# Scores of two heads in nearly every place of an attention loop, with values beside them

## The chip, the cores and the metric

The kernel runs on one core of a Trainium2 chip. The metric is the device time of one execution, in microseconds (us). The kernel before takes 1787.1 us (median of 3 runs, 1787.08 to 1787.36). Smaller is better.

## What is computed

Eight batches of attention with 12 heads, 448 tokens and 64 values per head, then a feed-forward block. Everything is float32 at the surface.

```python
scores = (q @ k.T) / 8                         # per batch and head, 448 x 448
scores = einsum('bhij,hg->bgij', scores, w_pre)    # heads mixed before the softmax
attn = exp(scores - max); attn /= sum + 1e-9
attn = einsum('bhij,hg->bgij', attn, w_post)       # heads mixed after it
x = (attn @ v), heads side by side             # 3584 tokens x 768
h = x @ w_in                                   # 2048 wide
out = (h - tanh(h)) @ w_out
```

The heads are mixed before and after the softmax, so all 12 heads of a token must be together twice: once for `w_pre`, once for `w_post`.

## The kernel before, in words

The attention part is one long loop over **places** (`for p in range(NPL + 3)`, L832; 180 of them). A batch is cut into four **blocks** of query tokens (120, 120, 120 and 88), 32 blocks in all. A block is cut into **groups** of 10 tokens with their 12 heads (120 rows of 128); a place handles two groups.

In every place TensorE (PE) does the same frame. **Premix** (`premix`, L513, matmuls L521) multiplies the gathered scores of the two groups with `w_pre` into the two PSUM banks of `ps_p`. **Mix** (`mix`, L548, matmuls L560) multiplies the exponentials of the place before with the scaled `w_post` into the two banks of `ps_o`, of which there is one copy only. Around these stand: VectorE (DVE) takes the row maximum (L530); ScalarE (ACT) the exponential with the row sum (L532); DVE forms the reciprocal of the sums (`norm`, L541 and L542) and GpSimd (POOL) scales `w_post` by it (`wr`, L543); ACT copies the mixed result to `at` at the start of the next place (L570, or L577 in two pieces where the two groups belong to different blocks or differ in size).

Between premix and mix a place may have **jobs**, from the table `todo`:

- `scores` (L467, matmuls L477): the scores of one **pair** of heads of a later block, 6 matmuls into two banks of `ps_m`; ACT copies one head to `s`, DVE the other (L482). Six pairs make a block.
- `values` (L590, matmuls L602): half of a finished block's `at` times v, 48 instructions into one bank of `ps_m`; DVE copies the result to `x` (L620). It needs all of the block's `at`.
- `prep_q` (L435, transposes L443): three transposes of q for a later block into one bank; ACT rounds them (`qh`, L456), DVE takes the rest (`ql`, L458). Two of these per block.
- `prep_k` (L409, transposes L417): four transposes of k into one bank; ACT (`kk`, L428) and DVE (L429) copy. Six per batch.
- `load_k`, `load_v`, `load_q`: entries in a list of DMAs that SyncE (SP) issues in later places.

`ps_m` has four banks in all. The order of a place's jobs on PE is fixed by `rank`: transposes, values, scores. On ACT and DVE a job's copies come behind the place's exponentials or row maxima; of DVE's, the score copies first, then what `then` and `last` hold (the rest of k and q, then the copy to `x`).

At the end of most places a few steps of the **narrowing** of the feed-forward weights are put in (`narrow_chunk`, L71; `Steps`, L113): 11 steps per chunk on DVE (L80 to L94), ACT (L82, L85, L102) and POOL (L96, L98, L104), 56 chunks. In ACT's order they stand between a place's score copies and the copy of the mix.

The rows of the scores reach the premix by a **gather** (L507, DMA L510): 120 rows of `s` from token order to group order, two per place, issued two places ahead, in a ring of six tiles.

All five engines run the instructions strictly in the order in which the code lists them (`in_order`). So the table `todo` sets what stands where. In the kernel before, each job of `scores` in the planner's list is two pairs, and the planner puts one job, scores or values, in a place, taking the other kind next where both are due. `prep_q` goes one place ahead of the block's first scores, both halves together; `prep_k` where no scores and no `prep_q` stand.

Behind the loop the feed-forward part streams the narrowed weights, with three matmuls per product of rounded parts (L257, L258, L262, L302 to L305). The change does not touch it.

## Time and profile before

| | |
|---|---|
| median of 3 runs | 1787.1 us |
| the profiled execution itself | 1788.9 us |
| its span, first to last instruction | 1787.2 us |
| mean granted TensorE clock | 0.993 |
| PE busy | 1751.0 us |
| DVE, ACT, POOL busy | 1128.3, 1000.5, 320.1 us |
| places of the attention loop | from 26.4 to about 838 us |

A row of the groups names line, engine, operation, output and inputs, the count, then the busy time and the mean of one, then the engine's idle time just before these instructions and what released it. A row of the timeline begins with start and duration in us; `x8` says how many instructions are merged; the bracket at its end is idle time before it and the releaser. A row of the windows has the stretch, its length, then busy time and count for PE, its weight loads, DVE, ACT and POOL, then the granted clock, the DMA share and GB/s. A float32 matmul is two instructions on PE in the trace and one row in the program's order; the ends of matmuls are modelled, so a section's cost is best read from start to start.

### The profile page before, as it was taken

To read this page: it belongs to the slowest core of one execution; us is meant where nothing else is said; L and a number is where in the kernel's file an instruction comes from. 1 tells how busy PE (TensorE), PEld (TensorE's weight loads), DVE (VectorE), ACT (ScalarE), POOL (GpSimd) and SP (SyncE) were. 2 spreads that over 40 slices of the span, in tenths; PEclk is the share of its full clock that TensorE was granted. 3 is DMA by queue.
4 is the path that set the end of the run, shared out by engine and by line. 5 is a ranking of instruction groups with operands and counts; after the bars stand their busy time and mean duration, and the time that the engine had idled before them with its cause. 6 is when DMAs were issued, how large, how long until landed. Compare 5 with 4: busy or idle time off the path is not lost.

```text
span 1787.2 us, 41382 instructions
## 1 busy us (share of the span) xinstructions
PE 1751.0 (98%) x16572; PEld 1425.6 (80%) x16572; DVE 1128.3 (63%) x2362; ACT 1000.5 (56%) x2051; POOL 320.1 (18%) x417
## 2 busy tenths in 40 slices
PE   8999999999999999999999999999999999999998
PEld 6777777777777777777888888888888888888887
DVE  5676777777777767664556566565565565655555
ACT  5777877777777776765343443433434434444333
POOL 1333333333333333321010010000000000000000
PEclk9999999999999999999999999999999999999999
DMA  8668687777967687565655655655656655655651
GB/s 176 204 196 216 194 236 224 217 215 215 249 203 218 215 213 220 178 202 216 255 207 194 248 193 207 241 193 214 229 197 216 224 208 204 228 217 190 230 194 36
DMA packets 232816, 372.32 MB, mean 208 GB/s; under 512 B 98992, under 2 KB 207536, under 8 KB 218288
## 3 DMA queue, kind: packets, MB, share of 16 engines
q1 hardware_dynamic: 231740, 368.45, 64.0%
q8 instruction: 131, 2.15, 0.5%
q10 hardware_dynamic: 884, 1.22, 0.2%
q14 instruction: 61, 0.50, 0.1%
HBM read 245.37 MB, written 47.19 MB: 164 GB/s over the span
## 4 chain that ended last, share of the span: by engine, by line
PE 87%; DMA 4%; ACT 4%; DVE 3%; issue 1%; POOL 0%; SPq 0%; ACTq 0%; DVEq 0%; POOLq 0%
PE ps_o L560 13%; PE ps_h L257 8%; PE ps_h L258 8%; PE ps_h L262 8%; PE ps_m L602 8%; PE ps_p L521 7%; PE ya L305 6%; PE ya L302 6%; PE ya L303 6%; PE ps_q L477 5%; PE yb L305 3%; PE yb L303 3%; PE yb L302 3%; DMA t<-s 2%; PE ps_m L443 1%
## 5 line engine op out<-in xcount | busy, mean ns | idle before, releaser
L560 PEld LDWEIGHTS ps_o<-wr,e 60*112 60x112 f32 (+1 forms) x5760 | 306.2, 176 | 44.3 <-POOL wr L543 21.8
L560 PE MATMUL ps_o<-wr,e 60*112 60x60 f32 (+1 forms) x5760 | 315.5, 259 | 14.3 <-POOL wr L543 7.7
L530 DVE TENSOR_REDUCE mx<-ps_p 128x1 f32<-128x448 f32 x360 | 207.7, 619 | 163.9 <-PE ps_p L521 163.7
L532 ACT ACTIVATE e<-ps_p,mx 128x448 f32<-128x448 f32 x360 | 225.7, 634 | 101.9 <-DVE mx L530 99.4
L289 ACT CAST gh<-r 128x512 fp32r<-128x512 f32 x112 | 69.6, 621 | 372.6 <-DVE r L282 372.6
L258 PE MATMUL ps_h<-xl,w 128*128 128x512 f32 x672 | 264.4, 393 | 0.0
L257 PE MATMUL ps_h<-xh,w 128*128 128x512 f32 x672 | 264.3, 393 | 0.0
L570 ACT COPY at<-ps_o 112x960 f32<-112x960 f32 x156 | 153.7, 985 | 93.8 <-PE ps_o L560 93.2
L247 POOL TENSOR_TENSOR xl<-rx,xh 128x512 fp32r<-128x512 f32 x38 | 55.6, 1464 | 731.2 <-ACT xh L246 731.2
L521 PE MATMUL ps_p<-t,wpre 60*64 60x448 f32 (+1 forms) x1440 | 180.8, 569 | 3.9 <-DMA t<-s 2.7
L305 PE MATMUL ya<-w,gl 128*128 128x512 f32 x448 | 177.0, 395 | 0.7 <-DVE gl L290 0.7
L278 DVE SCALAR_TENSOR_TENSOR r<-qa,ps_h 128x512 f32<-128x512 f32 x112 | 77.1, 688 | 159.2 <-ACT t L275 159.2
L302 PE MATMUL ya<-w,gh 128*128 128x512 f32 x448 | 174.8, 390 | 1.0 <-ACT gh L289 1.0
L303 PE MATMUL ya<-w,gh 128*128 128x512 f32 x448 | 174.8, 390 | 0.0
L602 PEld LDWEIGHTS ps_m<-at,vr 112*64 112x64 f32 x3072 | 147.5, 137 | 31.0 <-ACT at L577 10.9
L262 PE MATMUL ps_h<-xh,w 128*128 128x512 f32 x672 | 170.6, 389 | 0.0
L602 PE MATMUL ps_m<-at,vr 112*64 112x120 f32 (+1 forms) x3072 | 161.6, 261 | 8.4 <-ACT at L577 3.1
L272 ACT ACTIVATE u<-ps_h 128x512 f32<-128x512 f32 x112 | 67.0, 599 | 152.9 <-PE ps_h L262 152.9
L262 PEld LDWEIGHTS ps_h<-xh,w 128*128 128x128 f32 x672 | 126.3, 188 | 26.3
L258 PEld LDWEIGHTS ps_h<-xl,w 128*128 128x128 f32 x672 | 127.5, 190 | 23.7
L257 PEld LDWEIGHTS ps_h<-xh,w 128*128 128x128 f32 x672 | 127.4, 190 | 23.4
L543 POOL TENSOR_TENSOR wr<-wpost,zs 128x120 f32<-128x120 f32 x180 | 70.2, 390 | 402.9 <-DVE zs L542 293.6
(93 smaller groups left out, 3038.0 us busy)
## 6 DMA issues: line engine op xcount, KB each, us to landing
w<-ws SPq DMA_DIRECT2D x112, 1536.0 KB
t<-s SPq DMA_DIRECT2D x342, 210.0 KB
cr<-in_moe_w_in_dram SPq DMA_DIRECT2D x24, 512.0 KB
cr<-in_moe_w_out_dram SPq DMA_DIRECT2D x32, 384.0 KB
vr<-in_v_dram SPq DMA_DIRECT2D x24, 448.0 KB
kr<-in_k_dram SPq DMA_DIRECT2D x23, 448.0 KB
out_dram<-ob SPq DMA_DIRECT2D x24, 384.0 KB
qr<-in_q_dram SPq DMA_DIRECT2D x23, 360.0 KB
```

What stands on the lines that cost most here:

```text
L257: nc.tensor.matmul(ph, wh[:, fs], xh, start=(c == 0), stop=False)
L258: nc.tensor.matmul(ph, wh[:, fs], xl, start=False, stop=False)
L262: nc.tensor.matmul(ph, wl[:, fs], xh, start=False, stop=(c == NK - 1))
L302: nc.tensor.matmul(y, gh[:, tok], wh[:, es], start=first, stop=False)
L303: nc.tensor.matmul(y, gh[:, tok], wl[:, es], start=False, stop=False)
L305: nc.tensor.matmul(y, gl[:, tok], wh[:, es], start=False, stop=last)
L521: nc.tensor.matmul(pss[r][halves[j], :], wpre[k, :], ts[j][k, :], start=True, stop=True)
L530: nc.vector.tensor_reduce(out=mx, in_=ps, axis=AX.X, op=ALU.max, negate=True)
L532: nc.scalar.activation(e, ps, AF.Exp, bias=mx, scale=1.0, accum_out=zs[:, 0, r : r + 1])
L560: nc.tensor.matmul(ps[:CP, j, c * GP : (c + 1) * GP].rearrange("p (h i) -> p h i", i=GI)[:, :, r * GH : (r + 1) * GH], e[k, c * CP : (c + ...
L570: nc.scalar.copy(ats[i0][:, :, :, at : at + 2 * GI].rearrange("p c h (j i) -> p j (c h) i", j=2), ps[:CP, :, : NC * GP].rearrange("p j (x ...
L602: nc.tensor.matmul(pv[j * D : (j + 1) * D, r, :n], vt[:, j, c, :], ats[i][:, c, 2 * hp + j, :n], start=(c == 0), stop=(c == NC - 1),)
```

## The change

The planner that fills `todo` is rewritten. Scores are now placed pair by pair: for each block the pairs that are left are divided by the places that are left until they are due, rounded up. Values go into a place with no scores, or into one with one pair where the last values are two places back. The first blocks of a batch (but the very first) get their values two places later than the others. Transposes go wherever fewer than four banks of `ps_m` are taken; the two halves of `prep_q` may stand in different places. The first load of v for a batch waits until the place behind the last values of the batch before.

```diff
-        halved = []
+        def banks(p):
+
+            return sum({scores: 2, values: 1, prep_q: 1, prep_k: 1}.get(f, 0) for f, *a in todo[p])
+
+        at_s, at_v = {}, {}
+        due_s, due_v = [], []
         for i in range(len(blocks)):

             f0, f1, f2 = first[i : i + 3]
             if i + 1 < len(blocks):
-                lo = max(0, (f0 - 1) // 2 - 1)
-                hi = f1 // 2 - 3
-                for x in range(0 if i else 1, 3):
-                    e = lo + 2 * x if lo + 4 <= hi else lo + (hi - lo) * x // 2
-                    halved.append((e if i else x - 1, hi, "s", i + 1, x))
-            for x in range(2):
-                halved.append(((f1 - 1) // 2 + 2, f2 // 2 + 1 if f2 < NG else NPL + 7, "v", i, x))
...
+                lo, hi = max(0, (f0 - 1) // 2 - 1), f1 // 2 - 3
+                due_s += [(lo, hi, i + 1, hp) for hp in range(0 if i else 2, NP)]
+
+            lo = (f1 - 1) // 2 + (4 if i and i % NM == 0 else 2)
+            due_v += [(lo, f2 // 2 + 1 if f2 < NG else NPL + 7, i, x) for x in range(2)]
+        p, apart = 0, 2
+        while due_s or due_v:
+            now_s = 0
+            if due_s and due_s[0][0] <= p:
+                _, hi, i, _ = due_s[0]
+                left = sum(x[2] == i for x in due_s)
+                assert p <= hi, (p, hi, i)
+                now_s = -(-left // (hi - p + 1))
+                for _ in range(now_s):
+                    _, _, i, hp = due_s.pop(0)
+                    at_s[i, hp] = p
+                    at_place(p, scores, i, hp)
+            if due_v and due_v[0][0] <= p:
+                _, hi, i, x = due_v[0]
+                assert p <= hi, (p, hi, i)
+                if p + (1 - x) >= hi or now_s == 0 or now_s == 1 and apart >= 2:
+                    due_v.pop(0)
+                    at_v[i, x] = p
+                    at_place(p, values, i, x)
+                    apart = 0
+            apart += 1
             p += 1
...
             if b and m == 0:
+
+                p = max(p0 + 4, at_v[i - 1, 1] + 1)
+                assert p + 4 < at_v[i, 0], (p, at_v[i, 0])
                 for hq in range(NP // 2):
-                    at_place(p0 + 4 + hq, load_v, b, hq)
+                    at_place(p + hq, load_v, b, hq)
...
                 for r in range(2):
-                    while any(f is scores or f is prep_q for f, *a in todo[o]):
+                    while banks(o) > 3:
                         o += 1
                     at_place(o, prep_k, b, 2 * hq + r)
...
+        last_q = 0
+        for i in range(len(blocks)):
+            if i + 2 < len(blocks):
+                p = at_s[i + 2, 0]
+                for t in (1, 0):
+                    p -= t
+                    while banks(p) > 3:
+                        p -= 1
+                    at_place(p, prep_q, i + 2, t)
```

What this moves is read from the order of the instructions. The first place is PE in places 28 and 29, the start of the second batch. Before:

```order
L521 MATMUL ps_p<-t,wpre 64x448 x4
L417 MATMUL ps_m<-ident,kr 128x112 x8
L560 MATMUL ps_o<-wr,e 112x12x5 x16
L521 MATMUL ps_p<-t,wpre 64x448 x4
L477 MATMUL ps_q<-kk,qh 120x448 x4
L477 MATMUL ps_q<-kk,ql 120x448 x2
L477 MATMUL ps_q<-kk,qh 120x448 x4
L477 MATMUL ps_q<-kk,ql 120x448 x2
L560 MATMUL ps_o<-wr,e 112x12x5 x16
```

And with the change:

```order
L521 MATMUL ps_p<-t,wpre 64x448 x4
L417 MATMUL ps_m<-ident,kr 128x112 x8
L477 MATMUL ps_q<-kk,qh 120x448 x4
L477 MATMUL ps_q<-kk,ql 120x448 x2
L560 MATMUL ps_o<-wr,e 112x12x5 x16
L521 MATMUL ps_p<-t,wpre 64x448 x4
L477 MATMUL ps_q<-kk,qh 120x448 x4
L477 MATMUL ps_q<-kk,ql 120x448 x2
L560 MATMUL ps_o<-wr,e 112x12x5 x16
```

One of the two pairs (a row of four and a row of two matmuls) has moved ahead by a place, beside the k transposes; places 30 and 31 are then like 29, with one pair each and no values, where before place 30 had values.

The second is PE in places 18 and 19, where the third block of the first batch has just been mixed. Before:

```order
L521 MATMUL ps_p<-t,wpre 64x448 x4
L560 MATMUL ps_o<-wr,e 112x12x5 x16
L521 MATMUL ps_p<-t,wpre 64x448 x4
L477 MATMUL ps_q<-kk,qh 120x448 x4
L477 MATMUL ps_q<-kk,ql 120x448 x2
L477 MATMUL ps_q<-kk,qh 120x448 x4
L477 MATMUL ps_q<-kk,ql 120x448 x2
L560 MATMUL ps_o<-wr,e 112x12x5 x16
```

With the change:

```order
L521 MATMUL ps_p<-t,wpre 64x448 x4
L477 MATMUL ps_q<-kk,qh 120x448 x4
L477 MATMUL ps_q<-kk,ql 120x448 x2
L560 MATMUL ps_o<-wr,e 112x12x5 x16
L521 MATMUL ps_p<-t,wpre 64x448 x4
L602 MATMUL ps_m<-at,vr 64x120 x24
L477 MATMUL ps_q<-kk,qh 120x448 x4
L477 MATMUL ps_q<-kk,ql 120x448 x2
L560 MATMUL ps_o<-wr,e 112x12x5 x16
```

The empty place 18 has got a pair, and the values, which stood in place 20 behind six q transposes, now stand in 19, directly behind the premix and ahead of a pair.

The third is DVE in a place with values and q transposes. Before (place 43):

```order
L530 TENSOR_REDUCE mx<-ps_p 128x1 x2
L80 TENSOR_SCALAR cm<-cr 128x384
L458 SCALAR_TENSOR_TENSOR ql<-ps_m,qh 128x3x120 x2
L620 COPY x<-ps_m 128x3x12x10
L541 TENSOR_SCALAR zs<-zs 128x1 x2
L542 RECIPROCAL zs<-zs 128x2
```

With the change (place 42):

```order
L530 TENSOR_REDUCE mx<-ps_p 128x1 x2
L482 COPY s<-ps_q 120x448
L89 SCALAR_TENSOR_TENSOR cr<-cm,cs 128x384
L94 TENSOR_SCALAR cs<-cr 128x384
L458 SCALAR_TENSOR_TENSOR ql<-ps_m,qh 128x3x120
L620 COPY x<-ps_m 128x3x12x10
L541 TENSOR_SCALAR zs<-zs 128x1 x2
L542 RECIPROCAL zs<-zs 128x2
```

A score copy, which waits for matmuls that stand behind the values, has come ahead of the narrowing, `ql`, `x` and the sums. The narrowing's steps are at the same places in both kernels.

More of the change, by code (lines that the diff above doesn't have):

```diff
@@ L760, in kernel_body @@
             if i + 1 < len(blocks):
-                lo = max(0, (f0 - 1) // 2 - 1)
-                hi = f1 // 2 - 3
-                for x in range(0 if i else 1, 3):
-                    e = lo + 2 * x if lo + 4 <= hi else lo + (hi - lo) * x // 2
-                    halved.append((e if i else x - 1, hi, "s", i + 1, x))
-            for x in range(2):
-                halved.append(((f1 - 1) // 2 + 2, f2 // 2 + 1 if f2 < NG else NPL + 7, "v", i, x))
-        at_s, p, kind = {}, 0, None
-        while halved:
-            ready = sorted((x for x in halved if x[0] <= p), key=lambda x: (x[1], x[3:]))
-            if ready:
-                x = ready[0]
-                assert p <= x[1], (p, x)
-                other = [y for y in ready if y[2] != kind]
-                if x[2] == kind and other and x[1] > p + 1:
-                    x = other[0]
-                halved.remove(x)
-                _, _, kind, i, n = x
-                if kind == "s":
-                    at_s[i, n] = p
-                    for hp in (2 * n, 2 * n + 1):
-                        at_place(p, scores, i, hp)
-                else:
-                    at_place(p, values, i, n)
+                lo, hi = max(0, (f0 - 1) // 2 - 1), f1 // 2 - 3
[23 more added lines that the diff above has]
+            apart += 1
             p += 1
@@ L788, in kernel_body @@
             p0 = first[i] // 2
-            if i + 2 < len(blocks):
-                p = at_s[i + 2, 0] - 1
-                at_place(p, prep_q, i + 2, 0)
-                at_place(p, prep_q, i + 2, 1)
-                if i + 3 < len(blocks):
-                    at_place(p + 1, load_q, i + 3)
             if b and m == 0:
+                p = max(p0 + 4, at_v[i - 1, 1] + 1)
+                assert p + 4 < at_v[i, 0], (p, at_v[i, 0])
                 for hq in range(NP // 2):
-                    at_place(p0 + 4 + hq, load_v, b, hq)
+                    at_place(p + hq, load_v, b, hq)
         for b in range(1, B):
@@ L807, in kernel_body @@
                 if hq > KB - 4:
-                    o = max(o, at_s[blocks.index((b - 1, 3)), hq - 1 - (KB - 4)] + 1)
+                    o = max(o, at_s[blocks.index((b - 1, 3)), 2 * (hq - 1 - (KB - 4)) + 1] + 1)
                 for r in range(2):
-                    while any(f is scores or f is prep_q for f, *a in todo[o]):
+                    while banks(o) > 3:
                         o += 1
@@ L814, in kernel_body @@
                 done.append(o)
-                assert o < at_s[blocks.index((b, 0)), hq], (b, hq)
+                assert o < at_s[blocks.index((b, 0)), 2 * hq], (b, hq)
+        last_q = 0
[7 more added lines that the diff above has]
+                    at_place(p, prep_q, i + 2, t)
+                    last_q = max(p, last_q) if t == 0 else p
+                assert p > at_s.get((i, NP - 1), 0), p
+                p = last_q
+                if i + 3 < len(blocks):
+                    at_place(p + 1, load_q, i + 3)
         rank = {prep_k: 0, prep_q: 0, values: 1, scores: 2}
         for x in todo.values():
-            x.sort(key=lambda job: rank.get(job[0], 3))
+            x.sort(key=lambda job: (rank.get(job[0], 3), job[2] if job[0] is prep_q else 0))
         def hidden_0():
```

## The prediction

> **What bounds the kernel now.** I read the page first, then the groups of TensorE's instructions, then a window over the places of the attention loop, then the timeline of single places.

> ```profile
> PE 1751.0 (98%) x16572; PEld 1425.6 (80%) x16572; DVE 1128.3 (63%) x2362; ACT 1000.5 (56%) x2051; POOL 320.1 (18%) x417
> PE 87%; DMA 4%; ACT 4%; DVE 3%; issue 1%; POOL 0%; SPq 0%; ACTq 0%; DVEq 0%; POOLq 0%
> ```

> TensorE (PE) is the engine of the chain: 98% busy, 87% of the chain. The change adds and removes no matmul, so it can only move PE's waits, the little that a section costs to start, and the clock. The waits are in the window of the 180 places, which the change rewrites; everything behind it (the feed-forward part, about 950 us) is untouched.

> ```profile
> 26.41:838.20 811.79, 788.23 (x11556) 609.74 (x11556) 569.35 (x1538) 601.13 (x1371) 256.87 (x348) 0.99 0.72 211
> ...
> L560 PE MATMUL ps_o<-wr,e 60*112 60x60 f32 (+1 forms) x5760 | 315.5, 259 | 14.3 <-POOL wr L543 7.7 <-ACT at L570 6.0 <-POOL cl L104 0.3
> L521 PE MATMUL ps_p<-t,wpre 60*64 60x448 f32 (+1 forms) x1440 | 180.8, 569 | 3.9 <-DMA t<-s 2.7 <-ACT at L570 1.0
> L602 PE MATMUL ps_m<-at,vr 112*64 112x120 f32 (+1 forms) x2976 | 157.7, 262 | 8.4 <-ACT at L577 3.1 <-ACT at L570 2.7 <-DMA vr<-in_v_dram 2.4
> ```

> In 811.8 us PE is idle 23.6 us. By group (the rows of the attention part, idle before each): 14.3 us before the mix, 8.4 before the values, 3.9 before the premix (its first 1.6, and a little at the end, lie outside the window). That is all there is to win, a little over 1% of the time, and the same three lines are where a loss would stand.

> A place with four heads of scores, then an empty one, on PE (start, duration):

> ```profile
> 510.17 0.98 PE L521 MATMUL ps_p<-t,wpre 60*64 60x448 f32 x8
> 511.09 0.67 PE L477 MATMUL ps_q<-kk,qh 64*120 64x448 f32 x4
> ...
> 511.79 0.56 PE L477 MATMUL ps_q<-kk,qh 64*120 64x448 f32 x4
> ...
> 512.40 1.69 PE L560 MATMUL ps_o<-wr,e 60*112 60x60 f32 x32
> 514.02 0.98 PE L521 MATMUL ps_p<-t,wpre 60*64 60x448 f32 x8
> 516.34 1.78 PE L560 MATMUL ps_o<-wr,e 60*112 60x60 f32 x32 [1.33 <-POOL wr L543]
> 518.05 0.98 PE L521 MATMUL ps_p<-t,wpre 60*64 60x448 f32 x8
> ```

> From start to start: premix 0.92, first pair of heads 0.70, second pair 0.61, mix 1.62; the whole place 3.85. In the empty place behind it the mix could have begun 0.99 after the premix (516.34 - 514.02 less the wait of 1.33) and lasts 1.71: PE has 2.70 of work there and took 4.03.

> **The change part by part.**

> *PE's own work.* A place with one pair (two heads) should take 0.92 + 0.70 + 1.62 = 3.24. The program order has 92 places with two pairs before; with the change 26 with two and 131 with one. Scores: 131 x 0.70 + 26 x 1.31 - 92 x 1.31 = +5.2. The mix behind scores is 0.09 shorter than behind nothing or behind values, in 65 more places: -5.9. Only 3 of 14 empty places stay (premix 0.07 shorter elsewhere): -0.8. Split transposes start some 20 more sections; between 0 and the 0.09 by which a first pair exceeds a second, I take 0.05: +1.0. Sum -0.5, which I count as 0. If a lone pair cost 0.61 it would be -12; at 0.75, +6.5. The first pair is the nearest row, so 0.

> *The mix in the old light places.* 23 places without values behind another such place (13 empty, 10 with two k transposes) carry nearly all of the 14.3 us, 0.62 each. Each gets one pair, 0.70 later mix: those below that wait nothing, the 1.33 above and a 1.50 at 107.5 (below) keep 0.6 and 0.8, and two or three more like them keep some. I leave 4.5: **-9.8**. Bounds -14.3 and -6.

> *New light places behind light places.* The program order now has 50 of them, 27 more, because scores that stood alone between values places have been spread over all. What limits such a place is ScalarE (ACT), which works in order:

> ```profile
> 513.18 0.96 ACT L482 COPY s<-ps_q 120x448 f32<-120x448 f32 x2
> ...
> 517.03 0.51 ACT L102 CAST cs<-cm 128x384 fp32r<-128x384 f32 x1
> 517.43 0.53 ACT L82 ACTIVATE cm<-cm 128x384 f32<-128x384 f32 x1
> 517.85 0.55 ACT L85 ACTIVATE cr<-cr 128x384 f32<-128x384 int32 x1
> 518.29 0.96 ACT L570 COPY at<-ps_o 112x960 f32<-112x960 f32 x1
> ```

> The score copies start 3.01 after the place's premix (513.18 - 510.17), once both exponentials are through. One copy is 0.48, so ACT is free at 3.49, 0.25 into the next place of 3.24. The narrowing of the weights then takes 0.42 per operation (517.03 to 517.43 to 517.85), and the copy of the last mix 0.96 plus 0.1 to hand over (an estimate here and below): done 1.31 + 0.42 n into the place. PE wants to mix at 1.62. So n = 0 waits nothing, n = 1 0.1 (0.2 with the 512-wide chunks), n = 2 0.6, n = 3 1.0. The order, the same in both kernels, has 71 places with n = 0, 43 with one, 46 with two, 11 with three: (43 x 0.2 + 46 x 0.6 + 11 x 1.0) / 171 = 0.28. With the GpSimd product (7.7 of the 14.3) on top 0.32 x 27 = 8.6; a place that has waited gives ACT the time back, so **+7**. Bounds +2 (only n = 3 counts) and +17 (0.62 each, as in today's light places).

> *Values.*

> ```profile
> 391.46 0.98 PE L417 MATMUL ps_m<-ident,kr 112*128 112x112 f32 x8
> 392.38 2.68 PE L602 MATMUL ps_m<-at,vr 112*64 112x120 f32 x48
> ```

> Values in a block's first possible place read the mix that was just copied. Where 8 transposes (0.92) stand ahead they wait for nothing, as here; bare, they wait:

> ```profile
> 135.63 1.59 PE L602 MATMUL ps_m<-at,vr 112*64 112x88 f32 x36 [1.04 <-ACT at L577]
> ```

> Before, 21 blocks begin their values there, 11 of them behind 8 transposes, 10 bare. Now 24 do: 14 bare and 10 behind 3 or 4 transposes, and the place ahead is shorter (3.24 against 3.85), so ACT is later. Ready at 0.92, copy done at 1.31 + 0.42 n, or some 0.4 sooner where only half a place belongs to the block: 0.75 bare and 0.35 behind a few transposes, 14 x 0.75 + 10 x 0.35 = 14; less the time given back, 12.8. Gone are the 5.8 of ACT and the 2.4 of vr (the first blocks of a batch now begin two places later): **+4.6**. Bounds -4 (as today without vr) and +9.

> *VectorE's tail in places with values and one pair* (44 of them, none before):

> ```profile
> 503.86 0.97 DVE L458 SCALAR_TENSOR_TENSOR ql<-ps_m,qh 128x360 fp32r<-128x360 f32 x2 [0.49 <-ACT qh L456]
> 504.74 0.79 DVE L620 COPY x<-ps_m 128x360 f32<-128x360 f32 x1
> 505.38 0.18 DVE L541 TENSOR_SCALAR zs<-zs 128x1 f32<-128x1 f32 x2
> 505.60 0.17 DVE L542 RECIPROCAL zs<-zs 128x2 f32<-128x2 f32 x1
> ...
> 508.45 1.15 DVE L482 COPY s<-ps_q 120x448 f32<-120x448 f32 x2
> 509.52 0.35 DVE L87 TENSOR_SCALAR cs<-cr 128x384 int32<-128x384 int32 x1
> 509.97 0.56 DVE L89 SCALAR_TENSOR_TENSOR cr<-cm,cs 128x384 int32<-128x384 int32 x1
> ...
> 511.00 0.39 POOL L543 TENSOR_TENSOR wr<-wpost,zs 128x120 f32<-128x120 f32 x1 [3.47 <-DVE zs L542]
> ```

> The score copy now comes last on PE and first on DVE, and narrowing, ql, x, zs and wr queue behind it. From the end of the scores to the next mix PE needs 1.62 + 0.92 + 0.70 = 3.24. DVE and POOL need 0.1 + 0.58 + 0.8 + 0.4 + 0.5 = 2.4, with ql 2.9, plus about 0.45 per narrowing operation (0.35 and 0.56 above). By the order of these 44 places 15 exceed it, by 0.25 on average: 3.5, **+2.5** after give-back. Bounds 0 and +8.

> *Gathers.*

> ```profile
> 167.02 0.98 PE L521 MATMUL ps_p<-t,wpre 60*64 60x448 f32 x8 [0.81 <-DMA t<-s]
> ```

> Late only where a batch's v loads share the queue. The loads now begin one to four places later, among the shortest places (five without values in a row), and the last scores of a block fall one place nearer to their first gather: **+1.5**, bounds -2 and +6.

> *The clock.*

> ```profile
> 107.52 1.78 PE L560 MATMUL ps_o<-wr,e 60*112 60x60 f32 x32 [1.50 <-ACT at L570]
> ...
> 105.00:109.20 4.20, 2.70 (x44) 1.89 (x40) 3.62 (x11) 3.95 (x9) 0.93 (x3) 1.00 1.02 217
> 109.20:114.65 5.45, 5.45 (x55) 3.76 (x52) 3.03 (x8) 3.18 (x7) 1.96 (x3) 0.69 0.44 160
> ```

> After a wait of 1.50 the granted clock is 0.69 and a place of 3.85 takes 5.45, 1.6 more. Fewer waits of that size: one such dip less, **-1.5**; bounds -5 and +3.

> [...]

> Sum: 0 - 9.8 + 7 + 4.6 + 2.5 + 1.5 - 1.5 = +4.3. On the span of 1787.2 that is 1791.5; the median of the runs shown is 1787.1, the profiled execution itself took 1788.9, so I count from 1787: **1791**.

> **Rivals.** (A) *Evened places win, not slower.* One pair in nearly every place gives the mix 0.70 of cover everywhere, ACT's lag is carried from place to place without a wait, and the values, with scores behind them, no longer idle. For it: the mix waits in 23 of 180 places only, and over the window ACT is busy 601 of 812 us and DVE 569, so both have room on average. Against it: the copy of the mix must pass between ACT's narrowing and the next mix, and the cover shrinks from 1.31 to 0.70 where scores stood. New light places at +2, values at -2, tail 0, gathers 0, clock -3: 0 - 9.8 + 2 - 2 - 3 = -12.8, about 1774. (B) *VectorE and the gathers decide*: where narrowing falls with ql and x, the next row maximum is late too, and the whole place shifts; and two places of 3.24 leave 6.5 us between a place's start and the premix that needs its gather, where mostly one of the two was longer. Tail +8, gathers +6, the rest as forecast: +14.3, about 1801. For it: the gathers are late today already (167.02); against it: DVE has room on average. It decides once more than a third of the 44 places run over by 0.5. (C) *Waits only change their line*: new light places at +5, values at +3, tail +2: -9.8 + 5 + 3 + 2 + 1.5 - 1.5 = +0.2, about 1787.

> **How the numbers follow.** A measurement of this kernel tells about 0.2% (3.6 us) from no change. Forecast 0.45, own range 1785 to 1798, of which 0.28 is slower by more than 0.2% and 0.17 within it; A 0.30, faster; B 0.15, slower; C 0.10, within. Faster 0.30, same 0.27, slower 0.43. The range reaches to A and a little past B, 1773 to 1804.

> **What would show it.** In the groups: idle before L560 12 to 18 us (A: under 8), before L602 10 to 14 with ACT as releaser and no vr (A: under 6), before L521 4 to 6 (B: over 8). A lone pair from start to start 0.70. Released by POOL wr behind places with values: 15 or so (B: over 25). The forecast is wrong if PE's sections themselves become cheaper (a lone pair at 0.60), or if ACT's narrowing slips into gaps that I have not counted.

## The result and the profile after

The changed kernel takes 1844.8 us (median of 4 runs, 1837.9 to 1851.2); the kernel before, on the same chip, 1787.2. The ratio is 1.031, with an interval of 1.026 to 1.036. That is slower by 57.6 us, where 4 had been forecast and 1804 was the end of the range. The profiled execution took 1837.9 with a span of 1836.1; it is compared here with the one of before (span 1787.2).

First the page of the changed kernel, busy time and the chain, then a window over the attention loop. The loop's end has moved from 838 to 887 us; the feed-forward part behind it lasts as long as before.

```profile
PE 1778.7 (97%) x16572; PEld 1437.3 (78%) x16572; DVE 1123.5 (61%) x2362; ACT 1003.1 (55%) x2051; POOL 317.9 (17%) x417
PE 84%; DMA 6%; ACT 3%; DVE 3%; issue 1%; SPq 1%; POOL 1%; ACTq 0%; POOLq 0%; DVEq 0%
26.41:887.00 860.59, 816.20 (x11536) 621.87 (x11538) 561.85 (x1534) 604.30 (x1371) 255.80 (x348) 0.96 0.68 199
```

PE is 27.7 us *busier*, with the same 16572 matmuls: at a lower granted clock the matmuls last longer here (a premix 1.77 us at 0.50 and 0.98 at 1.00, below), and the granted clock of the loop has gone from 0.99 to 0.96. The rest is waits. The groups of PE in the attention part:

```profile
L560 PE MATMUL ps_o<-wr,e 60*112 60x60 f32 (+1 forms) x5760 | 316.3, 260 | 20.7 <-POOL wr L543 16.2 <-ACT at L570 3.2 <-issue 1.0
L521 PE MATMUL ps_p<-t,wpre 60*64 60x448 f32 (+1 forms) x1440 | 184.3, 578 | 13.8 <-DMA t<-s 13.5 <-ACT e L532 0.2
L602 PE MATMUL ps_m<-at,vr 112*64 112x120 f32 (+1 forms) x3072 | 170.8, 270 | 11.3 <-ACT at L570 7.3 <-ACT at L577 3.9
L443 PE MATMUL ps_m<-ident,qr 120*128 120x120 f32 (+1 forms) x186 | 29.8, 288 | 1.6 <-DMA qr<-in_q_dram 1.6
```

Idle before the mix 14.3 -> 20.7, before the values 8.4 -> 11.3 (v is no longer waited for), before the premix 3.9 -> 13.8, nearly all of it for gathers (`t<-s`).

**Where the loss sits.** Many places behave as the prediction priced them. Some two thirds of what the places lost (33 of 53 us, each measured against such a place without a wait and at full clock) stand in the places 4 to 13 behind a batch's first one, in the batches after the first, where the v, k and q loads are issued. One such stretch, places 142 to 144, on PE (start, duration):

```profile
712.61 0.98 PE L521 MATMUL ps_p<-t,wpre 60*64 60x448 f32 x8
...
714.83 1.78 PE L560 MATMUL ps_o<-wr,e 60*112 60x60 f32 x32 [0.44 <-POOL wr L543]
720.63 1.77 PE L521 MATMUL ps_p<-t,wpre 60*64 60x448 f32 x8 [4.01 <-DMA t<-s]
...
722.96 1.10 PE L477 MATMUL ps_q<-kk,qh 64*120 64x448 f32 x4
...
724.23 3.10 PE L560 MATMUL ps_o<-wr,e 60*112 60x60 f32 x32
727.26 1.77 PE L521 MATMUL ps_p<-t,wpre 60*64 60x448 f32 x8
...
729.59 4.78 PE L602 MATMUL ps_m<-at,vr 112*64 112x120 f32 x48
...
735.00 1.69 PE L560 MATMUL ps_o<-wr,e 60*112 60x60 f32 x32
```

The premix of place 143 waits 4.01 for its gather. Behind it everything lasts nearly twice as long until the values are through: premix 1.77 for 0.98, mix 3.10 for 1.69. The same time in windows of 3.41 us (PE's busy time is the first number after the comma, the granted clock the third from the end, then DMA share and GB/s):

```profile
716.92:720.33 3.41, 0.00 (x0) 0.00 (x0) 0.00 (x0) 0.71 (x1) 2.23 (x3) 0.99 1.01 228
720.33:723.74 3.41, 3.11 (x15) 1.49 (x17) 1.16 (x2) 0.57 (x2) 0.00 (x0) 0.50 0.90 280
723.74:727.16 3.42, 3.42 (x36) 3.28 (x34) 1.92 (x7) 2.52 (x8) 1.35 (x2) 0.50 0.92 261
727.16:730.57 3.41, 3.41 (x23) 1.71 (x23) 1.16 (x2) 1.73 (x4) 0.27 (x1) 0.50 0.89 234
730.57:733.98 3.41, 3.41 (x38) 3.41 (x36) 0.00 (x0) 0.87 (x3) 0.00 (x0) 0.51 0.35 119
733.98:737.40 3.42, 3.42 (x54) 2.56 (x50) 2.06 (x5) 1.77 (x3) 0.00 (x0) 1.00 0.04 10
```

Four stretches at a granted clock of 0.50 or 0.51 follow the wait, half of 3.41 us lost in each: 6.8 us beside the 4.0 of the wait. In the loop the changed kernel has 19 such stretches, the kernel before 5. The DMA engines' share is 0.89 to 1.01 until 730.

Why the gather is late stands on SP, which issues all loads, stores and gathers in order:

```profile
691.87 1.71 SPq L510 DMA_DIRECT2D t<-s  x2
693.63 0.66 SPq L369 DMA_DIRECT2D kr<-in_k_dram  x1
700.23 1.62 SPq L510 DMA_DIRECT2D t<-s  x2
701.89 0.65 SPq L369 DMA_DIRECT2D kr<-in_k_dram  x1
702.64 0.86 SPq L369 DMA_DIRECT2D xs<-x  x1
703.55 2.27 SPq L369 DMA_DIRECT2D ws<-cs  x1
...
706.62 1.70 SPq L510 DMA_DIRECT2D t<-s  x2
708.37 0.48 SPq L369 DMA_DIRECT2D vr<-in_v_dram  x1
...
709.62 2.62 SPq L369 DMA_DIRECT2D cr<-in_moe_w_in_dram  x1
712.34 1.64 SPq L510 DMA_DIRECT2D t<-s  x2
```

SP issues nothing from 694.3 to 700.2: the gather at 700.23 belongs to the first place of block 25, and its scores, copied last, stand one place later than before. Behind it the k load, the store of x, the weight stores, v, q and a weight chunk come in one go, and the gathers for places 142 and 143 go out 2.4 and 4.0 us after the start of the place that issues them (140 and 141). In the profile of before they go out 1.0 and 0.7 us ahead of that start (658.14 and 662.74 there):

```profile
657.18 2.18 SPq L510 DMA_DIRECT2D t<-s  x2
...
662.02 1.64 SPq L510 DMA_DIRECT2D t<-s  x2
```

This is how the gathers of these places came to be issued late; whether the holding is what costs the time is another question, on which e1 and e6 below bear.

SP's waits on the score copies, before and after (in total, times, longest):

```profile
SPq L510 <- DVE s L482: 42.6, 20, 9.6
```

```profile
SPq L510 <- DVE s L482: 121.1, 29, 12.2
```

A late load also stopped VectorE, which works in order here. In place 52 the first step of a weight chunk reaches it before the chunk, it idles 3.84, and the mix behind it waits 5.25:

```profile
274.18 0.43 DVE L80 TENSOR_SCALAR cm<-cr 128x512 f32<-128x512 f32 x1 [3.84 <-DMA cr<-in_moe_w_in_dram]
```

Summed over the loop's 178 full places, against PE's own sections as the prediction priced them, the time above them is (in us, profiled executions; "rest" is what is neither a recorded wait nor clock):

| kernel | PE idle | lost to the clock | rest |
|---|---|---|---|
| before | 23.6 | 8.5 | 1.1 |
| after | 44.4 | 32.4 | 7.7 |
| difference | 20.8 | 23.9 | 6.6 |

Each row is one execution. The granted clock over the span varies from one execution to the next: from 0.985 to 0.997 in the 65 executions of the kernel before that were timed beside the runs below, 0.991 in the mean, and from 0.977 to 0.981 in the four of the changed kernel. As 0.01 of the clock is some 18 us lost (an estimate, 0.01 of the span), the two kernels differ clearly, but ten us more or less in the clock column, here and below, tell little.

### The profile page after: what moved, and what is told of

It is laid out like the page before. It is cut to its first block, busy times and chain, and to the rows that moved or that the text cites. A ratio compares the mean times of both kernels' runs of the same rounds, so it can differ in the third digit from the quotient of the medians.

```text
span 1836.1 us, 41367 instructions
## 1 busy us (share of the span) xinstructions
PE 1778.7 (97%) x16572; PEld 1437.3 (78%) x16572; DVE 1123.5 (61%) x2362; ACT 1003.1 (55%) x2051; POOL 317.9 (17%) x417
## 4 chain that ended last, share of the span: by engine, by line
PE 84%; DMA 6%; ACT 3%; DVE 3%; issue 1%; SPq 1%; POOL 1%; ACTq 0%; POOLq 0%; DVEq 0%
PE ps_o L560 11%; PE ps_m L602 9%; PE ps_h L258 8%; PE ps_h L257 8%; PE ps_h L262 8%; PE ps_p L521 7%; PE ya L305 6%; PE ps_q L477 5%; PE ya L302 5%; PE ya L303 5%; DMA t<-s 4%; PE yb L305 3%; PE yb L303 3%; PE yb L302 3%; PE ps_m L443 1%
## 5 line engine op out<-in xcount | busy, mean ns | idle before, releaser
L560 PEld LDWEIGHTS ps_o<-wr,e 60*112 60x112 f32 (+1 forms) x5760 | 312.7, 178 | 47.9 <-POOL wr L543 32.5
L560 PE MATMUL ps_o<-wr,e 60*112 60x60 f32 (+1 forms) x5760 | 316.3, 260 | 20.7 <-POOL wr L543 16.2
L521 PE MATMUL ps_p<-t,wpre 60*64 60x448 f32 (+1 forms) x1440 | 184.3, 578 | 13.8 <-DMA t<-s 13.5
L482 DVE COPY s<-ps_q 120x448 f32<-120x448 f32 (+1 forms) x192 | 116.5, 618 | 130.0 <-PE ps_q L477 128.9
L570 ACT COPY at<-ps_o 112x960 f32<-112x960 f32 x156 | 153.6, 985 | 57.4 <-PE ps_o L560 56.9
L602 PEld LDWEIGHTS ps_m<-at,vr 112*64 112x64 f32 x3072 | 157.2, 143 | 34.9 <-ACT at L570 11.5
L602 PE MATMUL ps_m<-at,vr 112*64 112x120 f32 (+1 forms) x3072 | 170.8, 270 | 11.3 <-ACT at L570 7.3
L262 PEld LDWEIGHTS ps_h<-xh,w 128*128 128x128 f32 x672 | 126.1, 188 | 26.2
L543 POOL TENSOR_TENSOR wr<-wpost,zs 128x120 f32<-128x120 f32 x180 | 69.8, 388 | 438.8 <-DVE zs L542 293.2
```

The lines of the kernel that those rows point to most:

```text
L262: nc.tensor.matmul(ph, wl[:, fs], xh, start=False, stop=(c == NK - 1))
L521: nc.tensor.matmul(pss[r][halves[j], :], wpre[k, :], ts[j][k, :], start=True, stop=True)
L560: nc.tensor.matmul(ps[:CP, j, c * GP : (c + 1) * GP].rearrange("p (h i) -> p h i", i=GI)[:, :, r * GH : (r + 1) * GH], e[k, c * CP : (c + ...
L570: nc.scalar.copy(ats[i0][:, :, :, at : at + 2 * GI].rearrange("p c h (j i) -> p j (c h) i", j=2), ps[:CP, :, : NC * GP].rearrange("p j (x ...
L602: nc.tensor.matmul(pv[j * D : (j + 1) * D, r, :n], vt[:, j, c, :], ats[i][:, c, 2 * hp + j, :n], start=(c == 0), stop=(c == NC - 1),)
```

## The experiments

Four theories stood. (1) Loads come too thick at a batch's start. (2) The order itself costs: bare values, one pair of cover. (3) The last scores are too near their gathers. (4), formed after the first runs: the clock, once lowered, does not come back behind places with one pair. The kernel before was timed beside every run; its median was between 1787 and 1795, so what is compared is the ratio to it. In the runs e1 to e4 inserted lines shift the line numbers by 3 to 6.

| run | median us | ratio to before | PE idle | clock | rest |
|---|---|---|---|---|---|
| changed kernel | 1844.8 | 1.031 (1.026 to 1.036) | 44.4 | 32.4 | 7.7 |
| e1, without later v loads | 1810.9 | 1.011 (1.006 to 1.015) | 29.9 | 13.7 | 10.6 |
| e5, before without later v loads | 1786.1 | 0.995 (0.993 to 0.997) | 21.0 | 15.1 | -1.4 |
| e6, last scores earlier | 1814.5 | 1.011 (1.007 to 1.014) | 33.1 | 22.2 | 5.6 |
| e7, k loads earlier | 1833.4 | 1.020 (1.014 to 1.025) | 41.4 | 27.3 | 10.3 |
| e8, and v loads apart | 1825.5 | 1.016 (1.010 to 1.022) | 35.5 | 32.4 | 8.1 |
| e11, e6 and e1 together | 1787.7 | 0.998 (0.996 to 1.000) | 23.4 | 11.9 | 6.7 |
| e13, scores two pairs again | 1795.2 | 1.000 (0.998 to 1.001) | 21.4 | 15.4 | 1.1 |
| e15, before with k loads earlier | 1783.6 | 0.994 (0.991 to 0.996) | 18.8 | 10.2 | -0.1 |

### Loads left out

```diff
         def load_v(b, hq):
+            if b:
+                sent[b, hq, "v"], vts[b, hq] = sent[0, hq, "v"], vts[0, hq]
+                return
```

> The changed kernel without the 21 v loads of the batches after the first (their values are computed from the first batch's v, so that part of the output is another). Theory 1, late transfers: the v loads, now issued among a batch's shortest places, make gathers and chunk loads late, PE waits over 1.5 us, and the clock drops; without them about half of the 57 us of loss goes: 1810 (1800 to 1820), idle before the premix 13.8 -> under 7. Theory 2, the arrangement itself (values bare behind shorter places, one pair of cover in each place): no more than the vr share, 1835 or over. Theory 3, the last scores of a block stand one place nearer to their gathers: 1830 or over, idle before the premix stays over 10.

> The kernel before without the v loads of the batches after the first (their part of the output is another). All theories: its wait on vr (2.4 us) goes and some of the 2.7 on gathers, 1783 (1781 to 1786). What the changed kernel lost with these loads (34 us) is then the change's own, and 1810.9 less this time, some 28, is what the new order costs without them.

e1 measured 1810.9, e5 1786.1. In the changed kernel the v loads cost 34 us, in the kernel before 0.5%, some 8. Idle before the premix, as theory 1 had it, in e1:

```profile
L524 PE MATMUL ps_p<-t,wpre 60*64 60x448 f32 (+1 forms) x1440 | 181.8, 571 | 3.6 <-DMA t<-s 3.4
L563 PE MATMUL ps_o<-wr,e 60*112 60x60 f32 (+1 forms) x5760 | 313.8, 259 | 17.8 <-POOL wr L546 13.9 <-ACT at L573 3.2 <-issue 0.4
```

There remain some 25 us between e1 and e5, so late loads are not all.

Next the weight chunks: their loads after the third were left out, with or without the v loads, in the changed kernel (e2, e3) and in the kernel before (e4).

```diff
+        turn[0] += 1
+        if len(kept) == 3:
+            return kept[turn[0] % 3][:, : n2 // 2], lambda places=0: True
+        kept.append(pool.tile([p, CW, 2], I32, name="cr", tag="cr", bufs=3))
```

> The changed kernel without the loads of weight chunks after the first three (narrowing runs over those three again and again, so the weights of the feed-forward part are others). Theory 1: the first narrowing operation never stands on VectorE for a late chunk, and gathers have less beside them: 1815 (1800 to 1825), idle before the mix 20.7 -> 15 or less. Theory 2: 1835 or over. Theory 3: 1830 or over.

> The changed kernel without both, the v loads after the first batch and the chunk loads after the first three. Theory 1: what the prediction summed without gathers and clock stays, 1790 to 1797, granted clock 0.99. Theory 2: over 1825. Theory 3: over 1825 with idle before the premix over 10.

> The kernel before without the same loads. Its waits on vr (2.4 us) and on gathers (2.7) go, and no more: 1780 to 1784 by all theories. The distance to the changed kernel without the loads is what the new order costs by itself: 8 to 14 by theory 1, over 40 by 2 and 3.

Measured: e2 1843.5 (1.026), e3 1827.3 (1.020, slower than e1 with *fewer* loads), e4 1786.2 (0.996). All three missed or say nothing: a chunk that counts as landed at once starts its steps sooner, and the narrowing lies elsewhere in 158 of 180 places (by VectorE's steps), with two chunks in step. These runs changed two things and settle neither. What e3 tells against is a simple "more bytes, more time".

### The last scores, and loads moved

```diff
-                lo, hi = max(0, (f0 - 1) // 2 - 1), f1 // 2 - 3
+                lo, hi = max(0, (f0 - 1) // 2 - 1), f1 // 2 - 4
```

> The changed kernel with the last scores of each block one place earlier (its pairs are spread over one place less). Theory 3, that the loss comes from scores too near their gathers: 1800 to 1815, idle before the premix under 6, SP's waits on the score copies 121 -> under 60. Theory 1, too many loads in too little time at a batch's start: these loads stay where they are, 1835 to 1850, idle before the premix over 9.

1814.5, as theory 3 had it in time, but not in the way. SP's waits on the score copies are gone, the late gathers are not:

```profile
SPq L510 <- DVE s L482: 12.3, 5, 9.8
L521 PE MATMUL ps_p<-t,wpre 60*64 60x448 f32 (+1 forms) x1440 | 182.3, 573 | 15.5 <-DMA t<-s 13.5 <-ACT at L570 1.3 <-ACT cm L82 0.4
L560 PE MATMUL ps_o<-wr,e 60*112 60x60 f32 (+1 forms) x5760 | 316.4, 260 | 12.8 <-POOL wr L543 10.1 <-ACT at L570 1.3 <-issue 0.6
```

Where the v loads are issued it still has places with one pair (140 to 143 of those above). The gain is in the mix (20.7 -> 12.8), the values (11.3 -> 7.9) and the clock. With one place less to spread over, the kernel has 57 places with two pairs for 26: the edit is also a step back towards the old order.

```diff
-                at_place(p, load_k, b, hq)
+                at_place(p - 6 * (b > 1 and hq < 2), load_k, b, hq)
```

and, in e8 alone,

```diff
-                    at_place(p + hq, load_v, b, hq)
+                    at_place(p + 2 * hq, load_v, b, hq)
```

> The changed kernel with the first two k loads of each batch but the second six places earlier; no instruction of PE moves. Theory 1: two of the seven loads in six places leave the crowded stretch (places 137 to 142 of batch 7, 26 us), 1825 (1818 to 1835), idle before the premix 13.8 -> 5 to 9. Theories 2 and 3: 1840 or over.

> The same, and the three v loads of a batch two places apart instead of one. Theory 1: nearly what leaving the v loads out gave (1810.9): 1815 (1808 to 1825), idle before the premix under 5, granted clock 0.988 or more. Theories 2 and 3: 1840 or over.

e7 1833.4 and e8 1825.5, ratios 1.020 and 1.016. Idle before the premix falls from 13.8 to 10.6 and 7.0, but in e8 the clock costs as much as ever (32.4), and its waits can be small: behind 1.1 us of waiting in place 29 it runs 17 us at half clock. Theory 1 has the direction, not the size.

> The changed kernel with the last scores one place earlier (1814.5 by itself) and without the later v loads (1810.9 by itself). If the two losses are different ones (loads at the batch's start; one pair per place elsewhere), the gains add: 1785 to 1795. If both took away the same loss, 1805 to 1812.

e11 (both edits above: scores earlier, no later v loads) measured 1787.7, 0.998. Together the two edits give 57 us, the whole loss; by themselves they gave 34 (e1) and 30 (e6), so the gains add but for some 7. Beside e5, the kernel before without these loads (0.995), 0.3% is left.

### Which part of the change

The scores were put back two pairs at a time in every other place; the new rules for values and transposes stay, and so do the five places without values at a batch's start. By these rules 12 of the 64 jobs of values and 50 of the 102 of transposes stand in another place than in the changed kernel, by one place (a few transposes by two); of the loads only the third k load of a batch moves, by one. The last pair of each block that the loop computes stands one place sooner than in the changed kernel:

```diff
-                now_s = -(-left // (hi - p + 1))
+                now_s = 2 if left % 2 == 0 and (at_s.get((i, NP - 1 - left)) != p - 1 or left // 2 > (hi - p) // 2) else 0
```

> The changed kernel with one part undone: scores again two pairs at a time in every other place; values and transposes stay where the change puts them, and the five places without values at a batch's start stay too. If one pair per place is what hurts (a short cover for each wait, and no stretch of 3.4 us full enough to raise the clock): 1788 to 1800, idle before the mix under 16. If the crowded loads hurt whatever the scores do: these places are hardly longer (three of 3.85 and two of 2.70, 17.0, against five of 3.24, 16.2), so the late gathers stay: 1815 to 1835, idle before the premix over 8.

1795.2 beside 1795.3 for the kernel before: 0.9997 (0.9981 to 1.0013). Its groups, and SP's waits:

```profile
L560 PE MATMUL ps_o<-wr,e 60*112 60x60 f32 (+1 forms) x5760 | 317.9, 260 | 14.6 <-POOL wr L543 8.6 <-ACT at L570 3.5 <-POOL cl L104 1.2
L521 PE MATMUL ps_p<-t,wpre 60*64 60x448 f32 (+1 forms) x1440 | 182.7, 574 | 3.7 <-DMA t<-s 3.6
L602 PE MATMUL ps_m<-at,vr 112*64 112x120 f32 (+1 forms) x3072 | 161.7, 262 | 6.1 <-ACT at L570 4.2 <-ACT at L577 1.9
SPq L510 <- DVE s L482: 10.8, 6, 8.3
```

This run decides most. The whole loss belongs to the even spreading of the scores, of which the later last pair is a part; the new rules for values and transposes cost nothing together beside the old order of the scores. And the v loads, left in their places, do not hurt under two pairs. For the 34 us that e1 gave back it takes both, the loads and the single pairs; some 25 us (e1 against e5) the changed order costs without these loads.

Then the other part, the values of a batch's first block from their old place:

```diff
-            lo = (f1 - 1) // 2 + (4 if i and i % NM == 0 else 2)
+            lo = (f1 - 1) // 2 + 2
```

> The changed kernel with another part undone: the values of a batch's first block from their old place again, two places sooner, so that no five places without values stand in a row where the v loads are issued. By the crowded loads: the stretch of 26 us becomes 31, idle before the premix 13.8 -> under 7, less a wait on v of 2 to 5 before the values, 1818 to 1828. If one pair per place hurts alone: 1835 or over.

1849.2, 1.031: no gain. The premix waits only 4.1, but now the values wait for v:

```profile
L602 PE MATMUL ps_m<-at,vr 112*64 112x120 f32 (+1 forms) x3072 | 170.8, 269 | 34.8 <-DMA vr<-in_v_dram 20.9 <-ACT at L570 8.2 <-ACT at L577 5.1
```

The loads are as late as they were; only who waits for them has changed.

### The clock

GpSimd's product was computed eight times instead of once in five places, without the later v loads, in the changed kernel (e9) and in the kernel before (e10):

```diff
-            nc.gpsimd.tensor_mul(
+            for _ in range(8 if p in (28, 73, 95, 118, 163) else 1): nc.gpsimd.tensor_mul(
```

> The changed kernel without the later v loads (1810.9 as it was), with the product of wr computed eight times instead of once at places 28, 73, 95, 118 and 163 (each the fourth place ahead of a batch's first values, same result): the mix of places 29, 74, 96, 119 and 164 waits for some 2 us. Theory 4, the clock is decided over fixed stretches of 3.4 us by how much PE does in them, and places with one pair do too little to raise it again: each of the five waits is followed by a dip of 10.2 us that ends only with the values of place 32, 77, 99, 122 or 167. Time 1810.9 + 5 x (2.3 + 1.7 x 3) = 1848 (1838 to 1855). Rival, a dip's length goes by the wait alone: 3.4 to 6.8 us here as in the kernel before, 1810.9 + 5 x (2.3 + 2.5) = 1835.

> The kernel before without the later v loads (1786.1), with the same waits forced in the same places; behind them stand two pairs and values in turn. Theory 4: dips of 3.4 us, now and then 6.8, 1786 + 5 x (2.3 + 1.7 x 1.3) = 1808 (1803 to 1816). Rival: dips as long as in the changed kernel, the same distance between the two as without the forced waits (24.8 us).

e9 measured 1847.8 and e10 1810.9, close to theory 4 (1848 and 1808); the distance between the two grew from 24.8 to 37. As ratios to before it grew from 1.6% to 2.1%, and the four intervals together leave room for no growth at all, so the times alone do not tell theory 4 from its rival. One forced wait in windows of 3.41 us, e9 first, then e10 (place 74 in both):

```profile
386.94:390.36 3.42, 0.61 (x12) 0.61 (x14) 1.73 (x6) 1.25 (x5) 3.03 (x8) 1.00 0.92 233
390.36:393.77 3.41, 3.41 (x32) 2.22 (x30) 0.00 (x0) 1.03 (x2) 0.65 (x1) 0.50 1.00 262
...
404.01:407.42 3.41, 3.41 (x22) 1.70 (x22) 1.18 (x3) 1.44 (x2) 0.61 (x1) 0.50 0.16 63
407.42:410.84 3.42, 3.42 (x38) 3.42 (x38) 1.57 (x4) 1.44 (x6) 0.00 (x0) 0.50 0.67 241
410.84:414.25 3.41, 3.41 (x57) 2.48 (x54) 0.98 (x4) 0.86 (x1) 1.36 (x2) 1.00 0.01 2
```

```profile
365.23:368.64 3.41, 0.49 (x10) 0.49 (x10) 2.30 (x8) 1.65 (x6) 3.02 (x8) 1.00 0.87 242
368.64:372.05 3.41, 3.41 (x36) 2.50 (x32) 0.00 (x0) 0.99 (x2) 0.77 (x1) 0.50 1.04 273
372.05:375.47 3.42, 3.42 (x32) 2.83 (x30) 1.69 (x4) 1.78 (x6) 0.00 (x0) 0.50 0.30 117
375.47:378.88 3.41, 3.41 (x64) 2.83 (x60) 0.99 (x4) 0.45 (x1) 0.95 (x2) 1.00 0.12 41
```

With one pair per place the clock stays at 0.50 for six stretches, through two full places, until the values of place 77 have filled one; in the old order the values of place 75 end it after two. But place by place theory 4 is only half borne out. The five dips last 6.8, 20.5, 6.8, 10.2 and 6.8 us in e9 (10.2 on average; 10.2 had been expected for each), and 6.8, 6.8, none, 6.8 and 6.8 in e10. And the forced waits themselves are longer in e9 (3.42 on average against 2.58), probably since the second pair no longer covers them.

### What was tried for a faster kernel

The narrowing's steps dealt out unevenly, on top of the earlier last scores:

```diff
-                conv.place()
+                conv.place(1.6 if any(f is values for f, *a in todo[p]) else 0.66)
```

> The changed kernel with the last scores one place earlier, and with the narrowing's steps dealt out at 1.6 of their rate in places with values and 0.66 in the others. ACT, DVE and POOL then have less to do where the mix has only one pair of cover, and fewer chunk loads fall among the places of the v loads: by theories 1 and 4 the mix waits 12.8 -> 7 or less and time 1795 to 1805. If VectorE's tail behind values and a pair decides instead, the mix waits more than now and the time is 1815 or over.

1833.8 (1.023): the first branch missed, the second holds. The mix waits 18.9 instead of 12.8, and the premix 19.0, of which 15.6 for gathers. That the steps crowd onto VectorE and GpSimd in places with values fits this, but is not shown apart.

> The kernel before with the first two k loads of each batch but the second six places earlier. Leaving out the v loads there gave 0.5%; with two of seven loads moved out of the same stretch a part of that: 0.998 of before (0.995 to 1.000). If its late gathers come from the v loads alone, no change.

1783.6, 0.994 (0.991 to 0.996): the k edit of e7 in the kernel *before* makes it faster than both kernels. Its waits on v are gone and the gathers' are 1.6:

```profile
L521 PE MATMUL ps_p<-t,wpre 60*64 60x448 f32 (+1 forms) x1440 | 181.3, 570 | 1.6 <-DMA t<-s 1.6
L602 PE MATMUL ps_m<-at,vr 112*64 112x120 f32 (+1 forms) x3072 | 161.2, 261 | 6.0 <-ACT at L577 3.2 <-ACT at L570 2.7
```

The last runs exchanged two statements, so that a place's loads go out ahead of its gathers (e16 in the changed kernel, e17 in e15), and joined e13 with the earlier k loads (e18):

```diff
+            issue(6)
             for t in (2 * p + 4, 2 * p + 5):
                 if t < NG:
                     gather(t)
-            issue(6)
```

> The changed kernel with two statements exchanged: in each place the waiting loads are issued ahead of the two gathers; no instruction of PE, VectorE, ACT or GpSimd moves. Theory 3 in its narrower form (SP works in order; the gather of a block's first place waits up to 12 us for the last score copies, which stand one place later than before, and all loads behind it bunch up): the loads get out ahead of the held gather, idle before the premix 13.8 -> under 7, time 1815 to 1830. If the mere number of loads in the stretch is the cause, gathers behind loads come later still: 1845 or over.

> The kernel before with the k loads earlier (0.9937 of before by itself) and the loads issued ahead of the gathers. Its last scores stand where SP waits little (43 us in all), so there is little to win and a gather may come behind a load: 0.991 to 0.998 of before.

> The changed kernel with scores two pairs at a time again (0.9997 of before) and the k loads earlier. If what the k loads gave the kernel before holds here, where the values begin two places later and wait on no v load: 0.992 (0.988 to 0.996). If the late gathers were gone already by the later values: 0.998 to 1.000.

e16 took 1889.1 (1.052): theory 3 is far off, and the other branch, gathers later still, holds. e17 took 1824.0 (1.016), a miss for the same reason: its premix waits 25.7, 20.3 of it for gathers. e18 took 1791.2, 0.9985 (0.9965 to 1.0004), as its second branch had it. Under the same earlier k loads e15, the kernel before, has 0.9937 (0.9914 to 0.9959): there the change's other two parts do not seem free, but take away what the k loads gave. In e16 the gathers stand behind more loads:

```profile
L521 PE MATMUL ps_p<-t,wpre 60*64 60x448 f32 (+1 forms) x1440 | 197.6, 617 | 49.5 <-DMA t<-s 47.9 <-ACT at L570 1.1 <-ACT e L532 0.2
```

So it matters what stands ahead of a gather on SP. But the narrow form of theory 3, a held queue alone, does not hold, as e1 and e6 tell. In e1 SP is held as long as in the changed kernel (117.9 us) and the premix waits 3.6; in e6 it is held 12.3 us and the premix waits 15.5, of which 13.5 for gathers, as much as without the edit. SP's waits in e1:

```profile
SPq L513 <- DVE s L485: 117.9, 29, 10.0
```

The late gathers go with the v loads and with single pairs where these are issued: e1 lacks the loads, e13 the single pairs, e6 has both. Why single pairs make the gathers late there stays open, and so does what the later last pair costs by itself: no run has it without the spreading.

## Why the prediction was wrong, point by point

- **PE's own work, 0.** The section prices held (the order has 132 places with one pair, not 131, which is worth 0.7): of the 56 places of e1 that hold one pair and nothing else 28 do not wait, and 22 of these last 3.22 to 3.26 (forecast 3.24). What was missed is that a wait cost more than its idle time: where such a place waits, it lasts 3.23 plus the wait plus 0.24 to 0.28, in over 20 places. Most of the rest of 6.6 is this.
- **The mix and the tail, -9.8 + 7 + 2.5.** Forecast 14.0 idle before the mix, measured 20.7, of which one wait of 5.25 is the late chunk of place 52; released by POOL 16.2, where 15 was to be seen. Without the v loads 17.8. Roughly right; VectorE's tail, rival B's first half, did not decide.
- **Values, +4.6.** Forecast 10 to 14 with ACT as releaser and no v: 11.3, as forecast. One wait of 5.0 at place 7 hides in it, late through a weight chunk that held VectorE.
- **Gathers, +1.5, bounded by -2 and +6.** This step failed. Measured +9.9 before the premix alone, and the late loads reached PE by three other ways that had no term: the chunk steps on VectorE, the q transposes (L443, 0 -> 1.6), and the values of place 7. The text saw the v loads "among the shortest places" and the last scores one place nearer to their gather, and priced both by the waits of before; it did not ask what the loads do when they fall among single pairs. (The last scores stand later than before in 12 of 31 blocks, not in each.) With the v loads left out (e1) the premix waits 3.6, and with two pairs back (e13) 3.7, with all loads there. SP's queue, where the first gather of a block now holds the loads behind it (42.6 -> 121.1 us), was not followed either, but e1 and e6 show that the holding is not what decides.
- **The clock, -1.5, bounded by -5 and +3.** This step failed most: +23.9. It counted waits as long as the one at 107.5 and gave each one stretch of 1.6. The changed kernel has longer waits at the batch starts, and its dips last 8.1 us on average (19 stretches in 8 dips) where those of before last 4.3 (5 in 4): behind them come mixes and single pairs, not two pairs or values. With two pairs back (e13) 15.4 us go to the clock instead of 32.4.
- **The range.** Rival B reached the gathers with +6 and no clock. The bounds of both failed terms were drawn from rows of the kernel before, in which a gather is never more than a little late (0.81 us at 167.02, the longest wait of a premix for one behind the loop's first place); they say nothing of what happens once it is. B's reason for the gathers was the right one to look at: two places of 3.24 leave 6.5 us, and where the premix waits for a gather in the changed kernel, 6.5 to 10.0 us lie between the issue of the place's second gather and the premix (6.3 and 6.7 in the two such waits of e1).

## What to carry to other kernels

Where the order of work on the busiest engine is evened out, follow the queue that issues the transfers too: list for each place what it has to issue and which instruction holds it, before and after. Price a wait by what follows it: with its restart and with the clock, a wait of 4 us cost 11 here. Undoing one part of the change told in one run (e13) which part loses the time, which the runs on suspected causes had only narrowed; do that first. And hold each suspected cause against all runs: a queue that is held in a run without late gathers, and free in a run with them, is not their cause by itself.
